# A block of adaLN, spectral filter and SwiGLU on one core: three products instead of four in the spectral stage, in groups of four, with loads and warming matmuls reordered

## The chip, the cores and the metric

The kernel runs on one core of a Trainium2 chip. The metric is the device time of one execution in microseconds (us). Five runs of the kernel before gave a median of 291.14 us (290.09 to 292.46). The engines are TensorE (PE; its weight loads are PEld), VectorE (DVE), ScalarE (ACT), GpSimd (POOL) and SyncE (SP, whose queue SPq issues the DMAs).

## The reference

The input x has 2048 rows of 640 numbers in bf16. The layer has two halves, each behind a layer norm that is scaled and shifted per column by values computed from a vector c. The first half is a filter in the frequency domain, the second a SwiGLU network with 1728 hidden columns.

```python
mod = (_silu(c) @ w_mod).reshape(c.shape[0], 6, 1, -1)      # sa, ca, ga, sb, cb, gb
h = _layernorm(x, axis=-1) * (1 + ca) + sa
x = x + ga * irfft2(rfft2(h) * (w_r + 1j * w_i))
h = _layernorm(x, axis=-1) * (1 + cb) + sb
x = x + gb * ((_silu(h @ w_gate) * (h @ w_up)) @ w_down)
```

The two-dimensional transform has 2048 frequencies along the rows and 321 along the columns; w_r and w_i have that shape.

## The kernel before

The kernel is one straight program; each engine executes its own instructions in the order in which the program lists them, and all DMAs are issued from the SP queue in order.

**Tables and splitting.** The transforms are matmuls with tables built on the host. The 640 columns are split by their remainder r modulo 4, so that a column transform gives frequencies l = 0 to 80 and four combinations of the r give the rest. The 2048 rows are split as 128 x 16: row 16p + t sits on partition p in tile t. So the row transform is one of length 128 (tables G and H, with tile-dependent twiddles) and one of length 16 (tables KS2 and KI inside Ktab).

**Front (lines 220 to 376).** The SP queue issues c, the part of w_mod for ca, the table R, then x and G in pieces, and then the spectral weights. Each weight plane is needed twice: as it is (Wn), and mirrored in rows and columns (Wv); `flip` copies a plane reversed in rows into DRAM, and `load_rev` reads it back. TensorE runs 34 warming matmuls (lines 267 and 268) that nothing uses. Line 357 turns c into a column, line 358 applies silu, `mod_cols` (line 277) multiplies it with a part of w_mod in 25 matmuls with one moving column each, and lines 367 and 368 scale R with 1 + ca.

**Forward loop (lines 377 to 403).** For each of 16 tiles, `t1` transposes x (lines 304, 305), `stats` gets its moments by matmul (line 315), `dfwd` applies the column transform (lines 284, 287), `zout` subtracts the mean on VectorE (line 339), `gscale` scales G by the reciprocal standard deviation on GpSimd, and `s1`, two tiles later, applies the 128-point row transform (lines 348 to 351) into PSUM banks 6 and 7, from which ScalarE casts into A_sb (line 352). In iteration 12 the modulation sa is computed into bank 6, and in iteration 14 sixteen matmuls with a filled table SL (line 402) make SA, the contribution of the shift sa to row frequency 0. Lines 404 and 405 negate the w_i planes.

**Spectral stage (lines 408 to 580).** It goes over the 81 values of l in groups of 8 (some smaller). A_sb has to be transposed for each l: for two groups and the pair 0, 80 by TensorE (`t2_pe`, line 439), for the rest by DMA transposes of 16 l each (`t2_dma`, line 420). Three of those are issued at the start, the fourth in iteration 4, behind the modulation weights and two tables; `sa_add` (line 462, GpSimd) then adds SA. `stage_a` (line 470) applies the 16-point row transform with KS2, 128 columns per l, two PSUM banks per group, two groups in turn; VectorE multiplies the result with the weights in four instructions per group (line 482). The four real products of a complex product are kept apart in PP, and `stage_b` (line 502) sums and transposes them by two accumulating matmuls per l with the identity. ScalarE casts that to Y2 (line 508), `stage_c` (line 517) applies the inverse 16-point transform, and ScalarE writes Em or Er (lines 521 to 526). `rot` (lines 536, 537) makes the rotated copy on GpSimd, for the last groups on VectorE. `mods2` computes ga, gb (line 544), sb and cb (line 277) in iterations 4 to 8, and multiplies the table RI with ga on GpSimd (line 552). TensorE's order in iteration g is stage b of g, `mods2`, stage a of g + 2, stage c of g - 1.

**Inverse transform (lines 646 to 687) and FFN (lines 698 to 769).** `s1inv` needs all groups of E; line 670 adds the residual. The FFN goes in chunks of 2, 4, 4, 4 and 2 tiles; its gate and up weights are loaded into the place of Wn and Wv (line 591) once the last product is done.

Of the kernel before, what the change touches and what calls it, by code (L numbers as in the profile page):

```python
# [24 lines left out]
NWARM = 34  # L25
# [5 lines left out]
def _tables():  # L31

# [37 lines left out]
    KS2 = np.zeros((16, 2, 4, 2, 2, 16, 2))  # L70
    KI = np.zeros((3, 2, 2, 16, 2, 16, 4, 2))
    for m in range(4):
# [3 lines left out]
        for r in range(4):  # L76
# [3 lines left out]
            KS2[:, :, r, hl, :, :, mm] = M.transpose(2, 0, 1, 3)  # L80
# [8 lines left out]
    K = np.zeros((128, 4, 128))  # L89
    K[:, 0, :] = KS2.reshape(128, 128)  # L90
    for v in range(3):
        K[:, 1 + v, :] = KI[v].reshape(128, 128)
# [44 lines left out]
def adaln_block_kernel(ctx, tc, A_x, A_w_r, A_w_i, B_x, B_w_gate, B_w_up, B_w_down, c, w_mod, out):  # L137
# [24 lines left out]
    Ktab = const.tile([P, 4, 128], BF16, name="Ktab")  # L162
    KS2 = Ktab[:, 0, :]
# [41 lines left out]
    SL = rL.cut(0, [2, 4, 2, 128])  # L205
# [36 lines left out]
    Wflip = [flip(A_w_i, "wflip_i"), flip(A_w_r, "wflip_r")]  # L242

    def load_rev(plane, f):
        nc.sync.dma_start(Wv[:, plane, :, :], f[:].rearrange("k p l -> p k l"))
# [21 lines left out]
    for i in range(NWARM):  # L267
        nc.tensor.matmul(banks(0, 1, [128]), lhsT=ones[:], rhs=ones[:], start=True, stop=True)
# [25 lines left out]
    if True:  # L294
# [49 lines left out]
        def s1(t, Z, Gs):  # L344
# [7 lines left out]
            nc.scalar.copy(A_sb[:, :, t, :, :].rearrange("p l c r -> p c l r"),  # L352
                           aps[:, :, :324].rearrange("p c (r l) -> p c l r", r=4))

        cps = psum[:, 6, 0:NC5]
        for k in range(NC5):
            nc.tensor.matmul(cps[:, k:k + 1], lhsT=c_row[0:1, k * 128:(k + 1) * 128], rhs=one11[:], start=True, stop=True)
        nc.scalar.activation(sc_f[:], cps, ACT.Silu)
# [4 lines left out]
        mod_cols(mps, wm_ca, True)  # L363
        t1(0)
        nc.vector.tensor_scalar_add(one_p_ca[:], mps, 1.0)
        for r in range(4):
            nc.vector.tensor_scalar_mul(Rs[:, 0, r, :], Rp[:, 0, r, :], one_p_ca[:, r:r + 1])
        nc.vector.tensor_scalar_mul(Rs[:, 1], Rp[:, 1], one_p_ca[:, 4:5])
        t1(1)
        stats(0)  # L370
# [6 lines left out]
        for t in range(NT + 2):  # L377
# [11 lines left out]
            if t == 12:  # L389
                mps = psum[:, 6, 0:NC5]  # L390
                mod_cols(mps, wm_sa, True)
                nc.vector.tensor_copy(sa_col[:], mps)
                for v in range(2):
                    src = sa_col[:, 0:4] if v == 0 else sa_col[:, 4:5].to_broadcast([P, 4])
                    nc.vector.tensor_copy(_rev(SL, 1024 * v, [[257, 4], [132, 2], [8, NT]]),
                                          src.unsqueeze(2).unsqueeze(3).to_broadcast([P, 4, 2, NT]))
            if t == 14:
                sps = psum[:, 6, 0:NL]
                for i in range(16):
                    v, r, c2 = i // 8, i // 2 % 4, i % 2  # L400
                    b0 = 81 * c2
                    nc.tensor.matmul(sps, lhsT=SL[:, v, r, c2, :], rhs=Rp[:, v, r, b0:b0 + 81], start=(i == 0), stop=(i == 15))
                nc.vector.tensor_scalar_mul(SA[:], sps, float(P))
        nc.vector.tensor_scalar_mul(Wn[:, 0], Wn[:, 2], -1.0)
        nc.vector.tensor_scalar_mul(Wv[:, 0], Wv[:, 2], -1.0)


    Em = rE.cut(0, [2, 64, 128])
# [410 lines left out]
```

## Time and profile before

| | us |
|---|---|
| median of five runs | 291.14 |
| the profiled execution | 290.19 |
| its span, first to last instruction | 288.3 |
| TensorE busy | 266.8 (93%) |
| VectorE busy | 150.1 (52%) |
| ScalarE busy | 111.4 (39%) |
| GpSimd busy | 44.7 (16%) |

A timeline row reads: start in us, length in us, engine, line, operation, output <- input, count, and in brackets how long the engine had been idle and what ended that. Rows of one line that follow each other are merged. A row of the stretches view gives for each engine the busy time and the number of instructions, and then the clock that was granted to TensorE (1.00 is full), the busy share of the 16 DMA engines, and GB/s. A row of the groups view ends with the busy time, the mean length of one instruction in ns, and the idle time before.

### The profile page before, as it was taken

How to read it: one execution, taken by the hardware profiler on the slowest of the kernel's cores; microseconds unless marked ns; L12 is line 12 of the kernel's file. 1: busy time of each engine (PE TensorE's matmuls, PEld its weight loads, DVE VectorE, ACT ScalarE, POOL GpSimd, SP SyncE). 2: the span in 40 equal slices, each digit the busy share in tenths (PEclk: the TensorE clock that was granted, in tenths of full speed). 3: DMA queues.
4: the chain of work that ended last, by engine and by line, in shares of the span. 5: the costliest groups of instructions: out<-in, count | busy, mean ns of one | idle time of the engine just before them, and what ended most of it. 6: DMA issues, size and time to landing. Idle time of an engine off the chain costs nothing.

```text
span 288.3 us, 5475 instructions
## 1 busy us (share of the span) xinstructions
PE 266.8 (93%) x2222; PEld 184.7 (64%) x2222; DVE 150.1 (52%) x346; ACT 111.4 (39%) x198; POOL 44.7 (16%) x87
## 2 busy tenths in 40 slices
PE   6899986993959999999999999999999999999995
PEld 6688854872858888764444774444675444678883
DVE  1377768992546877943862323863322742422422
ACT  2468734772677778214223103322203223202310
POOL 4167741335340100200020000020000100000000
PEclk9999999999888999999999999999999999999999
DMA  6999967999959300051004011004001020011001
GB/s 232 366 286 309 314 174 140 247 394 169 321 177 389 76 2 5 3 114 32 2 11 79 24 48 32 0 2 92 22 31 49 0 48 0 0 48 50 3 0 45
DMA packets 41575, 31.27 MB, mean 108 GB/s; under 512 B 20815, under 2 KB 37070, under 8 KB 41422
## 3 DMA queue, kind: packets, MB, share of 16 engines
q1 hardware_dynamic: 41550, 30.93, 37.7%
q8 instruction: 17, 0.28, 0.4%
q14 instruction: 8, 0.07, 0.1%
HBM read 23.35 MB, written 4.72 MB: 97 GB/s over the span
## 4 chain that ended last, share of the span: by engine, by line
PE 65%; DMA 2%; DVE 1%; ACT 1%; issue 0%; ACTq 0%
PE psum L715 19%; PE psum L718 19%; PE psum L760 19%; PE psum L650 3%; DMA rW<-rL 2%; PE psum L665 2%; PE psum L668 1%; PE psum L705 1%; ACT rW L641 1%; PE psum L652 1%; DVE rA L728 1%; DVE rL L626 0%; DVE rE L722 0%; ACT rL L655 0%; DVE rE L763 0%
## 5 line engine op out<-in xcount | busy, mean ns | idle before, releaser
L718 PE MATMUL psum<-rW 128*128 128x512 bf16 (+1 forms) x325 | 66.9, 336 | 0.0
L715 PE MATMUL psum<-rW 128*128 128x512 bf16 (+1 forms) x325 | 66.9, 336 | 0.0
L721 ACT ACTIVATE rE<-psum 128x512 f32<-128x512 f32 (+1 forms) x65 | 33.2, 511 | 68.4 <-PE psum L715 68.3
L715 PEld LDWEIGHTS <-rW 128*128 128x128 bf16 x325 | 31.8, 98 | 24.5
L718 PEld LDWEIGHTS <-rW 128*128 128x128 bf16 x325 | 31.8, 98 | 24.5
L722 DVE TENSOR_TENSOR rX<-psum,rE 128x512 bf16<-128x512 f32 x26 | 17.9, 688 | 29.9 <-PE psum L718 28.4
L722 DVE TENSOR_TENSOR rE<-psum,rE 128x256 bf16<-128x256 f32 (+1 forms) x39 | 19.9, 511 | 24.6 <-PE psum L718 22.6
L765 DVE TENSOR_TENSOR rE<-psum,rM 128x640 bf16<-128x640 f32 x15 | 12.4, 824 | 38.3 <-PE psum L760 38.3
L760 PE MATMUL psum<-rA,rE 128*128 128x320 bf16 x224 | 31.2, 299 | 0.7 <-DVE rA L728 0.6
L760 PE MATMUL psum<-rA,rX 128*128 128x320 bf16 x224 | 30.8, 299 | 0.0
L482 DVE TENSOR_TENSOR rM<-psum,rW 128x512 bf16<-128x512 f32 (+3 forms) x48 | 25.5, 604 | 8.3 <-PE psum L470 8.3
L760 PEld LDWEIGHTS <-rE 128*128 128x128 bf16 x224 | 21.9, 98 | 9.6 <-issue 0.6
L760 PEld LDWEIGHTS <-rX 128*128 128x128 bf16 x224 | 21.9, 98 | 8.8
L622 POOL TENSOR_TENSOR rstd<-rstd,mhalf 128x4 f32<-128x4 f32 (+1 forms) x5 | 4.4, 885 | 138.8 <-DVE rstd L618 106.8
L707 ACT ACTIVATE rE<-psum 64x512 f32<-64x512 f32 (+1 forms) x5 | 2.5, 505 | 48.1 <-PE psum L705 48.1
L339 DVE SCALAR_TENSOR_TENSOR rE<-rE,msum,psum 128x648 bf16<-128x648 f32 x16 | 14.2, 889 | 5.7 <-PE psum L287 5.1
L502 PE MATMUL psum<-identb,rM 128*128 128x128 bf16 x162 | 14.3, 236 | 1.8 <-DVE rM L482 1.6
L670 DVE TENSOR_TENSOR rM<-psum,rX 128x640 f32<-128x640 f32 x16 | 12.9, 815 | 5.9 <-PE psum L668 5.8
L502 PEld LDWEIGHTS <-rM 128*128 128x128 bf16 x162 | 12.3, 150 | 2.9 <-DVE rM L482 2.8
L352 ACT CAST rA<-psum 128x648 bf16<-128x648 f32 x16 | 11.2, 699 | 7.0 <-PE psum L351 5.7
L307 ACT COPY rE<-psum 128x640 bf16<-128x640 bf16 x16 | 10.9, 693 | 6.7 <-PE psum L305 6.7
L508 ACT CAST rL<-psum 128x512 bf16<-128x512 f32 (+2 forms) x21 | 11.1, 577 | 5.2 <-PE psum L502 5.2
(122 smaller groups left out, 345.2 us busy)
## 6 DMA issues: line engine op xcount, KB each, us to landing
rM<-in_w_mod_dram SPq DMA_DIRECT2D x4, 800.0 KB, 6.2
out_dram<-rE SPq DMA_DIRECT2D x16, 160.0 KB, 1.8
rA<-in_B_w_down_dram SPq DMA_DIRECT2D x1, 2080.0 KB, 8.4
rX<-in_A_x_dram SPq DMA_DIRECT2D x3, 640.0 KB, 8.9
rM<-in_w_mod_dram SPq DMA_DIRECT2D x1, 1600.0 KB, 11.6
rW<-in_B_w_gate_dram SPq DMA_DIRECT2D x1, 1440.0 KB, 10.0
rW<-in_B_w_up_dram SPq DMA_DIRECT2D x1, 1440.0 KB
rE<-tab_G SPq DMA_DIRECT2D x4, 256.0 KB, 8.1
```

The costliest lines, as they stand in the source:

```text
L339: nc.vector.scalar_tensor_tensor(Z[:].rearrange("p (h r) n -> p h (r n)", h=2), Cb[:].rearrange("p (h r) n -> p h (r n)", h=2), msum[:, t: ...
L352: nc.scalar.copy(A_sb[:, :, t, :, :].rearrange("p l c r -> p c l r"), aps[:, :, :324].rearrange("p c (r l) -> p c l r", r=4))
L482: nc.vector.tensor_tensor(PP[:, cp, hl, :, :, :, :n], in0, in1, ALU.mult)
L502: nc.tensor.matmul(yps[:, i - lo, :], lhsT=PP[:, cp, :, :, :, :, i].rearrange("p h a k m -> p (h a k m)"), rhs=identb[:], start=(cp == 0 a ...
L508: nc.scalar.copy(Y2[:, lo:hi, :], yps[:, :hi - lo, :])
L670: nc.vector.tensor_tensor(x1[:, t, :].rearrange("p (m h r) -> p m h r", h=2, r=2), ops[:, :, 0:320].rearrange("p h (r m) -> p m h r", r=2) ...
L715: nc.tensor.matmul(gu[:, 0, 0:N], lhsT=Wgu[:, 0, c5, fc * 128:(fc + 1) * 128], rhs=h2T[:, :, c5, :], start=(c5 == 0), stop=(c5 == NC5 - 1))
L718: nc.tensor.matmul(gu[:, 1, 0:N], lhsT=Wgu[:, 1, c5, fc * 128:(fc + 1) * 128], rhs=h2T[:, :, c5, :], start=(c5 == 0), stop=(c5 == NC5 - 1))
L721: nc.scalar.activation(sg[:], gu[:, 0, 0:N], ACT.Silu)
L722: nc.vector.tensor_tensor(AT[:, fc, :], gu[:, 1, 0:N], sg[:], ALU.mult)
L760: nc.tensor.matmul(ops4[:, h, 0:320], lhsT=AT[:, fc, tl * 128:(tl + 1) * 128], rhs=Wd_sb[:, fc, h * 320:(h + 1) * 320], start=(fc == 0), s ...
L765: nc.vector.tensor_tensor(xo[:].rearrange("p (h m) -> p h m", h=2), ops4[:, :, 0:320], x1[:, t, :].rearrange("p (h m) -> p h m", h=2), ALU ...
```

## The change

- **Three products.** The complex product of a spectrum value X = a + ib with a weight W = wr + i wi is formed from three real products: KS2 now yields a, -(a + b) and b - a (192 columns per l), and Wn and Wv hold three planes, the sum wr + wi, wi and wr. Real and imaginary part are sums of two of the three, with one product shared. The two that are not shared go together through one full matmul with the identity; the shared one is added by two matmuls of 64 output rows each, into the lower and the upper half of the PSUM partitions. The sums of the planes are made by `wsum` on VectorE, for Wn in iterations 10 to 13 and after the forward loop, for Wv inside the spectral stage.
- **Groups of four** l instead of eight: 21 groups, VectorE multiplying in two instructions per group. In the loop, stage a of g + 2 now stands ahead of stage b of g. Every fourth eviction of E goes to VectorE, the rotation is done for two groups at once, and the last group's eviction and rotation are halved.
- **Transposes and loads.** All four DMA transposes are issued first, then RI and H, then the rest of w_mod; its part for ga is loaded before the forward loop ends. The natural-order weights are loaded ahead of the flips. Four groups and the pair 0, 80 are transposed by TensorE.
- **Front.** c is loaded from ScalarE's queue, tile 0 of x ahead of R; the 34 warming matmuls of 128 columns are replaced by `idle_pe`, 3, 8, 1 and 2 matmuls of 512 columns at four places.
- **Modulation.** The matmuls for sa and SA move to the end of the forward loop, with banks of their own, and the last two of `mods2` for gb and those for sb and cb to the end of the spectral stage.

The core of the diff:

```diff
-NWARM = 34
+IDLE = (3, 8, 1, 2)
...
+            KS2[:, :, r, 0, hl, :, mm] = M[:, :, 0]
+            KS2[:, :, r, 1, hl, :, mm] = -M[:, :, 0] - M[:, :, 1]
+            KS2[:, :, r, 2, hl, :, mm] = M[:, :, 1] - M[:, :, 0]
...
-    nc.sync.dma_start(c_row[:], c)
+    nc.scalar.dma_start(c_row[:], c)
     nc.sync.dma_start(wm_ca[:], wm_v[:, :, D:2 * D])
+    nc.sync.dma_start(x_sb[:, 0:1, :], x_v[:, 0:1, :])
     nc.sync.dma_start(Rp[:], R_dram)
-    nc.sync.dma_start(x_sb[:, 0:2, :], x_v[:, 0:2, :])
+    nc.sync.dma_start(x_sb[:, 1:2, :], x_v[:, 1:2, :])
...
-    nc.sync.dma_start(Wn[:, 2, :, :], wi_v[:, :, 0:NW])
-    load_rev(2, Wflip[0])
+    nc.sync.dma_start(Wn[:, 1, :, :], wi_v[:, :, 0:NW])
+    nc.sync.dma_start(Wn[:, 2, :, :], wr_v[:, :, 0:NW])
+    Wflip = [flip(A_w_i, "wflip_i"), flip(A_w_r, "wflip_r")]
+    nc.sync.dma_start(Ktab[:], K_dram)
     nc.sync.dma_start(wm_sa[:], wm_v[:, :, 0:D])
-    nc.sync.dma_start(Ktab[:], K_dram)
-    nc.sync.dma_start(Wn[:, 1, :, :], wr_v[:, :, 0:NW])
-    load_rev(1, Wflip[1])
+    for i in range(2):
+        nc.sync.dma_start(Wv[:, 1 + i, :, :], Wflip[i][:].rearrange("k p l -> p k l"))
+    nc.sync.dma_start(wm_r[:, :, 0, :], wm_m[:, :, 0, :])
...
+    def idle_pe(n):
+        for i in range(n):
+            nc.tensor.matmul(banks(5, 1, [512]), lhsT=ones[:], rhs=ones[:].unsqueeze(1).to_broadcast([P, 4, 128]),
+                             start=True, stop=True)
...
+        def wsum(W, lo, hi, eng):
+            off = lo if W is Wn else NW - hi
...
+            eng.tensor_tensor(v[0], v[2], v[1], ALU.add)
...
+            if 10 <= t < 14:
+                wsum(Wn, 16 * t - 160, 16 * t - 144, nc.vector)
...
-        nc.vector.tensor_scalar_mul(Wn[:, 0], Wn[:, 2], -1.0)
-        nc.vector.tensor_scalar_mul(Wv[:, 0], Wv[:, 2], -1.0)
...
-        for bi in range(3):
+        for bi in range(4):
             t2_dma(bi)
...
         def stage_a(g):
-            xps = banks(2 + 2 * (g % 2), 2, [8, 128])
+            xps = banks(2 + 2 * (g % 2), 2, [4, 256])
...
-                nc.tensor.matmul(xps[:, i, :], lhsT=B2[:, j, :], rhs=KS2, start=True, stop=True)
+                nc.tensor.matmul(xps[:, i, 0:192], lhsT=B2[:, j, :], rhs=KS2, start=True, stop=True)
...
+                nc.vector.tensor_tensor(PP[:, :, hl], xv[:, :, hl], in1, ALU.mult)
...
+        def stage_b(g, PP):
+            yps = banks(g % 2, 1, [4, 128])
+            for i in range(n):
+                nc.tensor.matmul(yps[:, i, :], lhsT=_rev(PP, 64 * n + i, [[n, 128]]), rhs=identb[:], start=(i == 0), stop=False)
+            for i in range(n):
+                for a in range(2):
+                    nc.tensor.matmul(yps[64 * a:64 * a + 64, i, :], lhsT=_rev(PP, i, [[n, 64]]), rhs=identb[:], start=False,
+                                     stop=(i == n - 1))
...
+                if g % 4 == 3:
+                    nc.vector.tensor_copy(Ev, ev)
+                else:
+                    nc.scalar.copy(Ev, ev)
...
         for g in range(NG + 1):
+            if g + 2 < NG:
+                PPs[g + 2] = stage_a(g + 2)
+            sa_add(g + 4)
+            if g < NG:
+                Y2s[g] = stage_b(g, PPs.pop(g))
+            if g in (0, 2):
+                wsum(Wv, 16 * g, 16 * g + 32, nc.vector)
+            if 5 <= g < 7:
+                mods2(g - 5, 6 + g % 2)
             if g >= 1:
                 stage_c(g - 1, Y2s.pop(g - 1))
-                rot(groups[g - 1], nc.gpsimd if g < NG - 2 else nc.vector)
+            if g == NG - 2:
+                mods2(2, 2 + 2 * (NG % 2))
+            if g == NG - 1:
+                mods2(3, 3 + 2 * (NG % 2))
+        mods2(4, 2 + 2 * (NG % 2))
```

More of the change, by code (lines that the diff above doesn't have):

```diff
@@ L266, in adaln_block_kernel @@
     nc.scalar.activation(warm[:], warm[:], ACT.Silu)
-    for i in range(NWARM):
-        nc.tensor.matmul(banks(0, 1, [128]), lhsT=ones[:], rhs=ones[:], start=True, stop=True)
+    def idle_pe(n):
+        for i in range(n):
+            nc.tensor.matmul(banks(5, 1, [512]), lhsT=ones[:], rhs=ones[:].unsqueeze(1).to_broadcast([P, 4, 128]),
+                             start=True, stop=True)
+    idle_pe(IDLE[0])
     def mod_cols(ps_ap, w_ap, radix):
@@ L509, in stage_y @@
+            Y2 = rL.cut(12288 + 1024 * (g % 2), [4, 128])
+            nc.scalar.copy(Y2[:, 0:n, :], yps[:, 0:n, :])
             return Y2
```

198 lines of the change are left out of this document (87 added, 111 removed).

## The prediction

> **What bounds the kernel now.** I read the page first (span, granted clock), then cut the span into stages with the stretches view, then followed the timeline of TensorE, VectorE and the SP queue through the stages that the change touches, and took prices from the groups view.
>
> ```profile
> span 288.3 us, 5475 instructions
> ```
> ```profile
> core 0: us, PE busy (x) PEld busy (x) DVE busy (x) ACT busy (x) POOL busy (x), PEclk, DMA share, GB/s
> 1.08:13.00 11.92, 10.19 (x102) 8.94 (x103) 2.24 (x17) 3.31 (x6) 2.72 (x3) 1.00 0.90 311
> 13.00:35.00 22.00, 20.96 (x247) 17.59 (x246) 16.70 (x66) 17.28 (x25) 15.24 (x32) 1.00 1.03 312
> 44.24:65.00 20.76, 17.61 (x238) 15.21 (x239) 19.15 (x34) 13.30 (x22) 6.10 (x14) 1.00 1.04 275
> 65.00:70.83 5.83, 1.14 (x10) 0.56 (x9) 1.15 (x2) 1.71 (x4) 3.06 (x4) 1.00 0.99 182
> 70.83:74.40 3.57, 3.57 (x34) 3.41 (x35) 2.48 (x4) 1.61 (x3) 1.90 (x4) 0.55 0.81 243
> 74.40:85.48 11.08, 7.64 (x135) 6.50 (x133) 5.38 (x18) 8.43 (x14) 4.59 (x8) 0.96 0.73 220
> 85.48:88.20 2.72, 2.72 (x24) 2.57 (x25) 0.00 (x0) 1.06 (x2) 0.00 (x0) 0.50 1.07 370
> 105.70:288.30 182.60, 178.42 (x1124) 109.47 (x1121) 81.36 (x164) 47.50 (x95) 5.58 (x8) 1.00 0.12 29
> ```
>
> The FFN after 105.70 (182.60 us, TensorE busy 178.42) is untouched, and I carry it over. The spectral stage runs from 44.24 to 85.48, 41.24 us. It has three parts: up to 65 us VectorE is busy 19.15 of 20.76 us, so the products of line 482 set the pace; then almost six microseconds in which TensorE and VectorE do next to nothing; then work at a granted clock of 0.55, and at 0.50 again from 85.48, when the inverse transform has begun.
>
> ```profile
> 44.26 7.72 SPq L420 DMA_TRANSPOSE rL<-rA  x3
> ```
> ```profile
> 55.59 12.77 SPq L420 DMA_TRANSPOSE rL<-rA  x1
> ```
> ```profile
> 64.14 1.16 PE L502 MATMUL psum<-identb,rM 128*128 128x128 bf16 x16
> 70.83 0.75 PE L470 MATMUL psum<-Ktab,rL 128*128 128x128 bf16 x8 [4.59 <-POOL rL L462]
> 72.23 1.91 PE L502 MATMUL psum<-identb,rM 128*128 128x128 bf16 x16
> ```
>
> These rows show the hole: the fourth DMA transpose reaches the SP queue at 55.59, behind the tables and modulation weights, and occupies it for 12.77 us; line 462 on GpSimd waits for its data, and TensorE for line 462. After the 4.59 us wait sixteen matmuls of line 502 take 1.91 us instead of 1.16.
>
> **Front.** The small load of c goes to ScalarE's queue, ahead of its table load; the first tile of x goes ahead of the table R; the 34 small warming matmuls become 3 + 8 + 1 + 2 of 512 columns, spread between the real ones.
>
> ```profile
> 1.08 3.81 PE L268 MATMUL psum<-ones 128*128 128x128 bf16 x34 [1.08 <-DVE warm L259]
> 5.88 0.96 PE L277 MATMUL psum<-sc_col,rM 128*128 128x1 bf16 x25 [0.77 <-DMA rM<-in_w_mod_dram]
> 7.55 0.61 PE L304 MATMUL psum<-identb,rX 128*128 128x128 bf16 x4 [0.70 <-DMA rX<-in_A_x_dram]
> 9.05 0.72 PE L315 MATMUL psum<-rE 128*128 128x129 bf16 x5 [0.25 <-ACT rE L307]
> 12.27 0.63 PE L304 MATMUL psum<-identb,rX 128*128 128x128 bf16 x4
> 13.00 0.44 PE L304 MATMUL psum<-identb,rX 128*128 128x128 bf16 x4
> ```
> ```profile
> out_dram<-rE SPq DMA_DIRECT2D x16, 160.0 KB, 1.8
> ```
>
> Four transposes take 0.63 us at 12.27 and 0.44 at 13.00: TensorE is at its slow pace until then, although the clock column reads 1.00. At that pace 128 columns cost 3.81/34 = 0.112 us, so 512 cost 0.45. A transfer of 160 KB lands 1.8 us after its issue, so c is there by about 3.0 and holds up nothing. If the pace stays slow: the 8 matmuls after the c columns end near 3.0 + 3.6 = 6.6, 0.7 later than line 277 started before; 0.96 + 0.45 + two transposed tiles at about 0.55 each + 0.9 put the first stats matmul at 10.0, one microsecond late; but what follows it up to 13.00 (3.95 us slow, about 2.0 at the full pace) then runs fast: 12.2 against 13.0, a gain of 0.8. If the unbroken run from 3.0 gives the full pace by 6.5: 6.5 + 0.8 + 0.2 + 0.6 + 0.45 = 8.6, plus 2.0 is 10.6, a gain of 2.4. I take 1.5, the middle. The forward loop after it is TensorE's (busy 20.96 of 22.00 us from 13 to 35, in which 13 tiles pass, 1.69 each), so the lead is carried on.
>
> The Trainium skill (TensorE: Matmul & The Clock Gate, "The HAM clock gate") says that full clock comes after one window of about 3.4 us of sustained activity and that the window runs freely; the grid of changes here (13.00, 74.4 and 88.2 lie 18 and 4 times 3.41 us apart) agrees. By it the gain would lie anywhere between my two ends, from run to run.
>
> **Tail of the forward loop.** Two inserts move out of iterations 12 and 14, and the two negations (lines 404, 405) go; four sums of 512 elements come into iterations 10 to 13 on VectorE, and one at the end.
>
> ```profile
> 35.02 0.93 PE L277 MATMUL psum<-sc_col,rM 128*128 128x1 bf16 x25 [0.23 <-ACT rA L352]
> ```
> ```profile
> 36.27 0.30 PE L348 MATMUL psum<-rE 128*128 128x324 bf16 x1
> ```
> ```profile
> 37.77 0.30 PE L348 MATMUL psum<-rE 128*128 128x324 bf16 x1 [0.23 <-ACT rA L352]
> ```
> ```profile
> 39.28 0.78 PE L402 MATMUL psum<-rE,rL 128*128 128x81 bf16 x16 [0.23 <-ACT rA L352]
> 40.47 0.30 PE L348 MATMUL psum<-rE 128*128 128x324 bf16 x1 [0.41 <-DVE SA L403]
> ```
> ```profile
> 43.73 1.22 DVE L405 TENSOR_SCALAR rW<-rW 128x4096 bf16<-128x4096 bf16 x1
> ```
> ```profile
> 46.79 1.29 DVE L482 TENSOR_TENSOR rM<-psum,rW 128x512 bf16<-128x512 f32 x2 [1.25 <-PE psum L470]
> ```
>
> Here one s1 follows the other at 1.50 us undisturbed, but at 2.70 around the SA matmuls, which shared banks 6 and 7 with s1: the insert costs 1.2, and that in iteration 12 (0.23 + 0.93) about as much. After, the mod columns (0.96) run in bank 0 while s1(14) waits for its bank anyway, exposing about 0.6; the SA matmuls (0.78) run while ScalarE casts s1(15), hidden but for some 0.3. So 2.4 - 0.6 - 0.3 = 1.5 gained; ends 0.5 and 2. The four sums find VectorE idle for (22.00 - 16.70)/13 = 0.4 us of each tile, about what one costs (below), and s1 takes what VectorE makes two tiles later. The sum ahead of SA's eviction (0.4) lies beside TensorE's SA matmuls.
>
> **Spectral stage.** Each l now takes three products instead of four: stage a moves 192 columns instead of 128, stage b takes one full matmul and two with 64 output rows instead of two full ones, groups are of 4 instead of 8, and all four DMA transposes go first.
>
> ```profile
> 54.34 0.61 PE L470 MATMUL psum<-Ktab,rL 128*128 128x128 bf16 x8
> ```
> ```profile
> 59.18 0.84 PE L544 MATMUL psum<-rM,sc_rep 128*128 128x320 bf16 x5
> ```
> ```profile
> L482 DVE TENSOR_TENSOR rM<-psum,rW 128x512 bf16<-128x512 f32 (+3 forms) x48 | 25.5, 604 | 8.3 <-PE psum L470 8.3
> ```
> ```profile
> 63.67 2.48 DVE L482 TENSOR_TENSOR rM<-psum,rW 128x512 bf16<-128x512 f32 x4 [0.32 <-PE psum L470]
> ```
> ```profile
> 75.37 1.42 DVE L482 TENSOR_TENSOR rM<-psum,rW 128x256 bf16<-128x256 f32 x4 [1.27 <-PE psum L470]
> ```
> ```profile
> 77.33 1.39 PE L277 MATMUL psum<-sc_col,rM 128*128 128x1 bf16 x50
> ```
> ```profile
> L728 DVE TENSOR_TENSOR rA<-rA,gb_bc 128x640 bf16<-128x640 bf16 (+1 forms) x14 | 6.6, 478 | 0.0
> ```
> ```profile
> L524 ACT CAST rE<-psum 128x512 bf16<-128x512 f32 x2 | 1.2, 596 | 0.0
> ```
>
> VectorE: 512 elements cost 0.62, 256 cost 0.355, so 384 cost 0.49; 21 groups of two, some smaller, are 19.9 us against 25.5 before. To it come the sums of Wv (544 and twice 1,024 elements; at the rate of line 728 about 0.4 + 2 x 0.75 = 1.9, at one element a cycle of line 482 2.8), and every fourth eviction of E (0.6 each, four before the last product): 19.9 + 1.9 + 2.4, and 0.3 for the piece of l = 80, make 24.5. So VectorE gains only about a microsecond over before.
>
> TensorE: eight matmuls of 128 columns take 0.61 with 0.15 of drain, 0.0575 each; five of 320 take 0.84, 0.136 each; 192 come out at 0.084. Line 502's sixteen give 0.0625. No row shows a 64-row matmul. Below, one could cost nothing beside its partner (0.031 each); above, its weight load could stand exposed, 0.15 more, by the row in the rivals. I take 0.0625, the price of the nearest row, the full one. Per l: 0.084 + 3 x 0.0625 + 0.0575 = 0.329, times 81 = 26.6 (before: 0.24, 19.4). With 18 transposes (1.2), the gate matmuls (4 x 0.68) and the mod columns, now at the end (1.39), 31.9 us. TensorE becomes the bound, by 31.9 against 24.5. Unhidden: from the first transpose through ScalarE's copy to the first product (before 46.79 - 44.24 = 2.55 us, with VectorE held up by line 405 to 44.95; now about 1.7), the wait for it (1.0), and at the end one Y eviction and one halved E eviction behind matmuls (0.8): 3.5 in all. 31.9 + 3.5 = 35.4 against 41.24: 5.8 gained, ends 3 and 9. The hole of 4.59 us goes because transposes 1 to 3 took about 2.6 us each (7.72 us of queue for three): the fourth lands some 14 us after the start, and its group is due at about 24. What is late next is TensorE itself. GpSimd's queue gets RI's two multiplications behind RI's landing; rotations behind them are due only at the end. The FFN's weights still wait for the last product and keep their distance to the FFN, which hangs on it too.
>
> **Inverse transform.** Its first 2.72 us ran at 0.50; with mod columns issued just ahead and no hole, full pace halves that: 1.2 gained, ends 0 and 1.4.
>
> **Sum.** 1.5 + 1.5 + 5.8 + 1.2 = 10.0: span 278.3, with 1.89 around it (290.19 - 288.3) 280.2. The profiled execution lies 0.95 below the median 291.14, so the median comes to 281.1, say 281.0.
>
> **Rivals.**
>
> ```profile
> L502 PEld LDWEIGHTS <-rM 128*128 128x128 bf16 x162 | 12.3, 150 | 2.9 <-DVE rM L482 2.8
> ```
> ```profile
> 30.38 4.32 SPq L245 DMA_DIRECT2D rW<-wflip_r  x1
> ```
> ```profile
> rW<-wflip_r SPq DMA_DIRECT2D x1, 0.5 KB, 11.8
> ```
> *Half matmuls expose their weight loads* (slower). If a 64-row matmul cannot start its load under its predecessor, each of the 162 adds up to the 0.150 us of the strided load: 24 us, 305. It decides from 0.062 us exposed per half (10.0/162). For it: nothing in this trace uses half the array. Against: line 502's loads, at 0.150 each, hide in a spacing of 0.0625. Chance 0.07.
>
> *The array drains at each change of shape.* Stage b changes from full to half and back in all 21 groups. A matmul of line 470 leaves 0.15 us behind its issue; two per group are 42 x 0.16 = 6.7 us: 287.7. Nothing in the trace excludes it. Chance 0.20. The Trainium skill (TensorEngine Tiling (Array Packing), "Key Properties") states that changing the tiling mode drains TensorE; the same page says that the two halves can run in parallel. No run here shows either.
>
> *Pairs run side by side.* Two halves for the price of one save 81 x 0.0625 = 5.1; the stage's 35.4 comes to 30.3, which VectorE allows (1.7 + 24.5, and some 2.7 for the last group's way through b, Y, c and E: 28.9): 276. Chance 0.15.
>
> *Data is late.* Wv's last load is issued at 30.38 and lands 11.8 later, at 42.2, as the queue is busy throughout (1.03 from 13 to 35); the new order starts 0.4 earlier and makes Wv wait for the same data; the stage would start at 41.2 and want Wv by 43. Another 800 KB is queued ahead of the transposes, so they may not go first in fact. If either slips 2 us: 283. Chance 0.08.
>
> **How the numbers follow.** The forecast has 0.50; its own range, from the ends above, is 277.5 to 285. About 0.5% (1.5 us) is what a measurement here can tell from no change. The range 275.5 to 288 takes in the pairs and the drain and leaves out the exposed loads and the far ends, some 0.17. Faster: 0.50 + 0.15 + 0.08 + most of the drain, 0.16 = 0.89; slower 0.07; same 0.04.
>
> **What would show it.** Right: no wait of line 462's successor over 1 us; stretch from the first transposes to the first inverse matmul 34 to 38 us, TensorE busy about 32 of it; VectorE with idle time before the products; clock 1.00 at the start of the inverse; the forward loop's end near 41.2. Wrong: half matmuls with starts over 0.1 apart or gaps of 0.15 around them; a product waiting for a DMA of rW; the first stats matmul after 10.2 with no faster pace behind it; an FFN longer than 182.6.

## The result and the profile after

The changed kernel takes 280.73 us, the median of 9 runs (279.90 to 282.04); the kernel before, in 15 runs beside it, 291.14. The ratio is 0.9645, with a 95% interval of 0.9622 to 0.9667. The profiled execution took 280.76 us, so it stands for the median. Of its page the first line:

```profile
span 279.0 us, 5649 instructions
```

The span fell by 9.3 us, from 288.3. The stretches view of the changed kernel shows where (columns as in the prediction's first view):

```profile
13.83:38.75 24.92, 24.22 (x280) 19.43 (x278) 20.00 (x71) 17.48 (x26) 17.92 (x37) 1.00 1.03 288
40.07:45.00 4.93, 2.03 (x27) 1.76 (x27) 1.82 (x6) 2.46 (x4) 0.78 (x4) 1.00 1.26 276
45.00:48.30 3.30, 3.30 (x32) 2.58 (x31) 3.23 (x7) 0.59 (x1) 0.00 (x0) 0.52 0.99 175
48.30:60.00 11.70, 10.60 (x153) 8.94 (x149) 8.97 (x19) 8.40 (x16) 5.05 (x8) 0.99 1.07 244
60.00:70.00 10.00, 10.00 (x159) 8.75 (x158) 8.89 (x19) 7.46 (x14) 6.25 (x12) 1.00 1.05 381
76.91:79.63 2.72, 2.52 (x43) 2.24 (x40) 1.06 (x6) 1.29 (x2) 0.40 (x1) 1.00 1.08 393
96.26:279.00 182.74, 178.43 (x1123) 109.47 (x1121) 81.39 (x164) 47.54 (x95) 5.59 (x8) 1.00 0.12 29
```

The reader is to see three things. Between 60 and 70 us TensorE is busy all the time and VectorE is not: the bound of the spectral stage has moved to TensorE. The stage's first eight microseconds are poor: TensorE works 2.03 of 4.93 us, and then 3.30 us at a granted clock of 0.52. And the inverse begins at clock 1.00, where it had 0.50. The stretch at 0.52 belongs to the profiled execution: in four of the nine the mean granted clock was 1.00, and these took 279.90 to 281.10 us, against 280.51 to 282.04 for the other five.

The timeline of the changed kernel gives the reason for the poor start, the order of loads on the SP queue, what GpSimd does, and one group in the steady state:

```profile
32.34 4.44 SPq L257 DMA_DIRECT2D rW<-wflip_r  x1
...
40.32 11.59 SPq L444 DMA_TRANSPOSE rL<-rA  x3
52.02 2.16 SPq L444 DMA_TRANSPOSE rM<-rA  x1
54.23 0.74 SPq L450 DMA_DIRECT2D rH<-tab_RI  x1
```
```profile
43.89 0.46 DVE L374 TENSOR_TENSOR rW<-rW 128x544 bf16<-128x544 bf16 x1 [1.44 <-DMA rW<-wflip_r]
45.00 0.69 PE L487 MATMUL psum<-Ktab,rM 128*128 128x192 bf16 x4 [2.23 <-DVE rM L498]
57.87 2.76 POOL L565 TENSOR_TENSOR rH<-rH,ga_bc 128x640 bf16<-128x640 bf16 x2 [3.13 <-DMA rH<-tab_RI]
61.66 0.27 POOL L479 TENSOR_TENSOR rL<-rL,SA 128x16 bf16<-128x16 bf16 x1
...
58.07 0.49 PE L487 MATMUL psum<-Ktab,rL 128*128 128x192 bf16 x4
58.40 0.39 PE L505 MATMUL psum<-identb,rM 128*128 128x128 bf16 x4
58.72 0.46 PE L508 MATMUL psum<-identb,rM 128*64 128x128 bf16 x8
59.11 0.40 PE L520 MATMUL psum<-Ktab,rL 128*128 128x128 bf16 x4
59.34 0.49 PE L487 MATMUL psum<-Ktab,rL 128*128 128x192 bf16 x4
```

VectorE needs the sum of the mirrored planes for the first group, and waits 1.44 us for the mirrored wr to land at 43.89; TensorE waits 2.23 us for the product behind it. The mirrored wr is issued at 32.34, where the kernel before issued it at 30.38, and takes about as long to land. A group of four takes from 58.07 to 59.34, 1.27 us, without a gap. The four-microsecond hole around the fourth block is gone.

The landmarks of all profiled kernels, read off TensorE's timeline (start of the first row transform of the forward loop, of the first transpose of the spectral stage, of the first inverse matmul; the stage is the difference of the last two), with the medians:

| kernel | first row transform | stage starts | inverse starts | stage | median us |
|---|---|---|---|---|---|
| before | 16.60 | 44.24 | 85.48 | 41.24 | 291.14 |
| changed | 13.83 | 40.07 | 76.91 | 36.84 | 280.73 |
| before, fourth transpose first | 16.98 | 45.16 | 88.40 | 43.24 | 292.93 |
| before, new front | 14.13 | 44.26 | 86.07 | 41.81 | 292.81 |
| before, both | 14.26 | 44.89 | 87.28 | 42.39 | 293.31 |
| before, hole gone | 16.59 | 44.54 | 81.42 | 36.88 | 286.39 |
| changed but four products | 14.13 | 40.65 | 78.70 | 38.05 | 283.18 |
| changed, tables late | 13.87 | 40.09 | 86.05 | 45.96 | 290.38 |
| changed, old front | 16.95 | 43.18 | 77.65 | 34.47 | 281.29 |
| changed, idle matmuls out | 14.86 | 41.08 | 76.72 | 35.64 | 280.84 |
| changed, flips first | 14.13 | 44.19 | 78.28 | 34.09 | 282.38 |
| changed, two full matmuls | 14.13 | 40.38 | 74.69 | 34.31 | 279.30 |
| flips first, sums late, two full | 14.19 | 40.28 | 74.72 | 34.44 | 277.68 |
| the same, gate late | 14.14 | 40.22 | 73.59 | 33.37 | 277.64 |

Kernels with the same front differ by up to 0.4 us in the first column (16.59 to 16.98 with the old one, 13.83 to 14.26 with the new one and its idle matmuls), so a landmark's difference of that size says little.

### The profile page after: what moved, and what is told of

Same layout as the page of the kernel before. It is cut to its first block, busy times and chain, and to the rows that moved or that the text cites. A ratio compares the mean times of both kernels' runs of the same rounds, so it can differ in the third digit from the quotient of the medians.

```text
span 279.0 us, 5649 instructions
## 1 busy us (share of the span) xinstructions
PE 266.8 (96%) x2283; PEld 181.6 (65%) x2283; DVE 149.8 (54%) x353; ACT 109.8 (39%) x202; POOL 46.0 (16%) x90
## 4 chain that ended last, share of the span: by engine, by line
PE 75%; DMA 9%; SPq 8%; DVE 3%; ACT 2%; issue 1%; ACTq 0%; DVEq 0%
PE psum L731 20%; PE psum L734 20%; PE psum L776 19%; DMA rW<-wflip_r 4%; SPq L252 3%; PE psum L508 3%; DMA rE<-tab_G 2%; PE psum L487 2%; PE psum L520 2%; SPq L244 2%; PE psum L666 2%; DMA rW<-rL 2%; PE psum L681 2%; PE psum L505 2%; SPq L242 1%; PE psum L684 1%
## 5 line engine op out<-in xcount | busy, mean ns | idle before, releaser
L731 PEld LDWEIGHTS <-rW 128*128 128x128 bf16 x325 | 31.8, 98 | 24.5
L734 PEld LDWEIGHTS <-rW 128*128 128x128 bf16 x325 | 31.8, 98 | 24.5
L498 DVE TENSOR_TENSOR rM<-psum,rW 128x384 bf16<-128x384 f32 (+2 forms) x42 | 20.9, 548 | 3.4 <-PE psum L487 3.3
L511 ACT CAST rL<-psum 128x512 bf16<-128x512 f32 (+2 forms) x21 | 12.0, 572 | 9.4 <-PE psum L508 9.2
L671 ACT CAST rL<-psum 128x640 bf16<-128x640 f32 x16 | 10.9, 690 | 5.1 <-PE psum L668 3.3
L364 ACT CAST rA<-psum 128x648 bf16<-128x648 f32 x15 | 10.5, 700 | 5.5 <-PE psum L361 4.2
L642 DVE TENSOR_SCALAR rL<-rM,st,rstd 128x640 bf16<-128x640 f32 x16 | 9.7, 625 | 0.5 <-POOL rstd L638 0.5
## 6 DMA issues: line engine op xcount, KB each, us to landing
rW<-in_B_w_up_dram SPq DMA_DIRECT2D x1, 1440.0 KB, 12.2
```

Of the source, the lines that this page charges most:

```text
L498: nc.vector.tensor_tensor(PP[:, :, hl], xv[:, :, hl], in1, ALU.mult)
L511: nc.scalar.copy(Y2[:, 0:n, :], yps[:, 0:n, :])
L671: nc.scalar.copy(VT[:], vps[:, 0:5, :])
L731: nc.tensor.matmul(gu[:, 0, 0:N], lhsT=Wgu[:, 0, c5, fc * 128:(fc + 1) * 128], rhs=h2T[:, :, c5, :], start=(c5 == 0), stop=(c5 == NC5 - 1))
L734: nc.tensor.matmul(gu[:, 1, 0:N], lhsT=Wgu[:, 1, c5, fc * 128:(fc + 1) * 128], rhs=h2T[:, :, c5, :], start=(c5 == 0), stop=(c5 == NC5 - 1))
```

## The experiments

My theory after the first look: the hole is worth its 4.6 us and the front its 2.8, so that most of the gain can be had with four products. The rival: the gain hangs on the three products. The kernel before had medians of 291.70, 291.61, 291.38 and 291.17 us in the four batches of runs.

### What the hole was

**The fourth transpose alone.** The kernel before, with the fourth DMA transpose issued right behind the first three; its block gets a place of its own, and the products two buffers instead of three.

```diff
-        for bi in range(3):
+        for bi in range(4):
             t2_dma(bi)
...
-            if g == 4:
-                t2_dma(3)
```

> The kernel before, with one thing changed: the fourth DMA transpose is issued right behind the first three, into a buffer of its own (the product buffers go from three to two to make room). Theory A (the hole and the slow stretch behind it were the cost of the old spectral stage, the number of products was not): 4.6 us of hole and 1.7 of slow pace go, some 0.8 at the start of the inverse: 284 to 285. Theory B (the old stage was bound by VectorE's four products, and the hole only hid part of that): VectorE and the later loads take up most of the room, 288 or more.

292.93 us, a ratio of 1.0024 (0.9991 to 1.0056): nothing. The timeline of this kernel:

```profile
70.08 2.74 POOL L552 TENSOR_TENSOR rH<-rH,ga_bc 128x640 bf16<-128x640 bf16 x2 [4.14 <-DMA rH<-tab_RI]
72.78 0.27 POOL L462 TENSOR_TENSOR rM<-rM,SA 128x16 bf16<-128x16 bf16 x1
73.10 1.03 PE L470 MATMUL psum<-Ktab,rM 128*128 128x128 bf16 x8 [4.49 <-POOL rM L462]
```

The block has long landed, but its addition (line 462) stands in GpSimd's queue behind the multiplication of RI (line 552), and that waits 4.14 us for RI, which is loaded behind all of the modulation weights. The same two rows of the kernel before:

```profile
66.19 2.74 POOL L552 TENSOR_TENSOR rH<-rH,ga_bc 128x640 bf16<-128x640 bf16 x2 [2.61 <-DMA rH<-tab_RI]
70.51 0.27 POOL L462 TENSOR_TENSOR rL<-rL,SA 128x16 bf16<-128x16 bf16 x1 [1.58 <-DMA rL<-rA]
```

There the block landed 1.58 us after line 552 was done. So the hole had two causes, one behind the other, and I had seen only the last.

**Both, front and hole.** The same with the new front.

```diff
-            if g == 4:
-                t2_dma(3)
...
-NWARM = 34
+IDLE = (3, 8, 1, 2)
```

> Both edits together on the kernel before, with four products in groups of eight and the old place of the SA matmuls. Theory A: the gains add, 291.1 - 6.5 - 2.8 = 282, within 1.5 us of the changed kernel, so the three products themselves bring next to nothing. Theory B: 286 or more, the rest being the products' own.

293.31 us, 1.0055 (1.0025 to 1.0085). The hole stood as before (TensorE waited 4.83 us for GpSimd at 72.45), and the front's lead did not reach the stage either.

**The addition moved forward.** The first experiment, with one change more: GpSimd adds to a block one group earlier, so ahead of line 552 in its queue.

```diff
-            sa_add(g + 1)
+            sa_add(g + 2)
```

> The first experiment again (fourth transpose issued right behind the first three), and GpSimd adds the mean's term to a block one group earlier in its queue, ahead of its two multiplications by the gate. Theory A (the hole of the kernel before was this addition's place in GpSimd's queue, behind a multiplication that waited for a table, and TensorE has no other wait there): TensorE's 4.5 us wait goes, about 287 us against 291.7. Theory B (GpSimd or VectorE is late anyway and the wait comes back at the next group or at the end of the stage): 290 or more.

286.39 us, 0.9818 (0.9787 to 0.9850), 5.2 us less than the kernel before. Its timeline:

```profile
60.23 0.27 POOL L462 TENSOR_TENSOR rM<-rM,SA 128x16 bf16<-128x16 bf16 x1
69.41 2.76 POOL L552 TENSOR_TENSOR rH<-rH,ga_bc 128x640 bf16<-128x640 bf16 x2 [4.08 <-DMA rH<-tab_RI]
67.82 0.61 PE L470 MATMUL psum<-Ktab,rM 128*128 128x128 bf16 x8
```

GpSimd still waits 4.08 us for RI, and nobody minds: TensorE takes the block at 67.82 without a wait. With four products in groups of eight the stage now takes 36.88 us, as long as the changed kernel's.

**The tables late.** The changed kernel, with RI and H loaded behind the modulation weights as before.

```diff
-        nc.sync.dma_start(RI[:], RI_dram)
-        nc.sync.dma_start(Htab[:], H_dram)
         nc.sync.dma_start(wm_r[:, :, 3, :], wm_m[:, :, 3, :])
         nc.sync.dma_start(wm_r[:, :, 1:3, :], wm_m[:, :, 1:3, :])
+        nc.sync.dma_start(RI[:], RI_dram)
+        nc.sync.dma_start(Htab[:], H_dram)
```

> The changed kernel with the two tables of the inverse (RI and H) loaded behind the modulation weights again, as in the kernel before. Theory A (GpSimd's queue is what counts: the addition to the third block stands behind the multiplications of RI, which would then wait for the table): RI lands some 7 us later, TensorE waits 4 us or more for a block, 284 to 287 us. Theory B (with all four transposes first and the additions four groups ahead the table's place does not matter): 280 to 281.5 us.

290.38 us, 0.9956 (0.9940 to 0.9973): with these two loads behind, 9.65 of the 10.4 us are lost. Timeline and one stretch of this kernel:

```profile
65.77 2.74 POOL L565 TENSOR_TENSOR rH<-rH,ga_bc 128x640 bf16<-128x640 bf16 x2 [10.91 <-DMA rH<-tab_RI]
69.54 0.27 POOL L479 TENSOR_TENSOR rL<-rL,SA 128x16 bf16<-128x16 bf16 x1
69.86 0.82 PE L487 MATMUL psum<-Ktab,rL 128*128 128x192 bf16 x4 [7.67 <-POOL rL L479]
```
```profile
69.86:72.65 2.79, 2.79 (x24) 2.36 (x25) 1.02 (x2) 0.88 (x2) 1.06 (x2) 0.50 1.12 334
```

TensorE waits 7.67 us and then works 2.79 us at half clock, which costs some 1.4 more: together the 9.1 us by which the stage grew. The forecast of 284 to 287 priced only the wait, and that too low. The gains do not add up one by one: the additions moved forward gave 5.2 us without any change to the tables. One edit takes the addition out from behind the wait for RI, the other shortens that wait.

### What became of the lead

**New front alone**, on the kernel before.

```diff
-NWARM = 34
+IDLE = (3, 8, 1, 2)
...
-    nc.sync.dma_start(c_row[:], c)
+    nc.scalar.dma_start(c_row[:], c)
...
+    nc.sync.dma_start(x_sb[:, 0:1, :], x_v[:, 0:1, :])
     nc.sync.dma_start(Rp[:], R_dram)
```

> The kernel before with the new front alone: c on ScalarE's queue, tile 0 of x ahead of the table R, 3 + 8 + 1 + 2 warming matmuls of 512 columns, the order of the scalings of R. If the lead of 2.8 us at the first row transform is carried through: 288.3. If the loads of the weights then hold the spectral stage up by as much, or the fourth transpose's queue does: 290 to 291.

292.81 us, 1.0027 (0.9994 to 1.0060). The first row transform starts 2.47 us earlier, the stage at the same time: in iteration 12 the lead is given back. From this kernel's timeline:

```profile
35.01 0.95 PE L283 MATMUL psum<-sc_col,rM 128*128 128x1 bf16 x25 [2.70 <-DMA rM<-in_w_mod_dram]
```

The matmuls for sa wait for their part of w_mod. The changed kernel has them in the last iteration, where the data are there.

**The idle matmuls out.** The changed kernel without the eight long matmuls behind the columns of c.

```diff
-IDLE = (3, 8, 1, 2)
+IDLE = (3, 0, 1, 2)
```

> The changed kernel without its eight long idle matmuls behind the columns of c, so that TensorE pauses between the first columns and the modulation columns. Theory A (the front's gain of 2.8 us comes from TensorE's unbroken work up to the full pace at about 4.2 us): the pace stays slow for up to 7 us more, the first row transform starts at 15 to 16.6 in place of 13.83, and the time is 281.7 to 283.5 against 280.7. Theory B (the gain comes from the early load of c and the order of the loads): first row transform at or before 14.2, 280 to 281.2 us.

280.84 us, 0.9629 (0.9598 to 0.9660). Timeline:

```profile
5.78 0.96 PE L287 MATMUL psum<-sc_col,rM 128*128 128x1 bf16 x25 [3.02 <-DMA rM<-in_w_mod_dram]
...
8.90 0.65 PE L325 MATMUL psum<-rE 128*128 128x129 bf16 x5
9.38 0.30 PE L294 MATMUL psum<-rE 128*128 128x324 bf16 x1
...
14.86 0.31 PE L358 MATMUL psum<-rE 128*128 128x324 bf16 x1
```

The full pace comes at about 9.3 us and the row transform at 14.86, 1.03 later than in the changed kernel: between the two theories, nearer to A. The time says B: the inverse starts at 76.72, as early as before. The stage begins later, finds the mirrored weights landed, and has neither the wait nor the slow stretch.

**The old front.** The front's loads and warming matmuls as before, in the changed kernel; only the order in which R is scaled stays.

```diff
-IDLE = (3, 8, 1, 2)
+NWARM = 34
...
-    nc.scalar.dma_start(c_row[:], c)
+    nc.sync.dma_start(c_row[:], c)
...
-    nc.sync.dma_start(x_sb[:, 0:1, :], x_v[:, 0:1, :])
     nc.sync.dma_start(Rp[:], R_dram)
```

> The changed kernel with the front of the kernel before (34 small warming matmuls, c on SP's queue, the first two tiles of x behind the table R). Theory A (the front's lead of 2.8 us is used up by the wait for the reversed weights, which land at 43.9 us whenever the loop ends): first row transform at about 16.6, stage start at about 42.8, no wait for the weights, first inverse matmul within 0.8 us of the changed kernel's 76.91, 280.5 to 282 us against 280.7. Theory B (the lead is kept): 283 to 284 us.

281.29 us, 0.9674 (0.9636 to 0.9713). The stage starts 3.1 us later than the changed kernel's and the inverse 0.74 later. Its stage as one stretch, and that of the changed kernel:

```profile
43.18:77.65 34.47, 31.55 (x493) 27.08 (x494) 26.64 (x57) 23.53 (x44) 16.21 (x31) 1.00 1.09 278
```
```profile
40.07:76.91 36.84, 32.84 (x493) 27.95 (x494) 27.01 (x57) 23.53 (x44) 16.19 (x31) 0.95 1.08 288
```

For the same 493 matmuls the changed kernel has 1.3 us more of busy time, at clock 0.95, and 1.1 us more of waiting: 2.4 us of the lead is paid back to the late load.

**Flips first.** The changed kernel with the mirrored copies issued ahead of the plain weights.

```diff
+    Wflip = [flip(A_w_i, "wflip_i"), flip(A_w_r, "wflip_r")]
     nc.sync.dma_start(Wn[:, 1, :, :], wi_v[:, :, 0:NW])
     nc.sync.dma_start(Wn[:, 2, :, :], wr_v[:, :, 0:NW])
-    Wflip = [flip(A_w_i, "wflip_i"), flip(A_w_r, "wflip_r")]
```

> The changed kernel with the three-part flips issued ahead of the natural-order weights, as in the kernel before; everything else as changed. If the order of the loads makes Wv late (the SP queue stands still until the second flip has landed): the wait of VectorE for Wv (1.4 us) and of TensorE behind it (2.2 us) go, and with them the slow stretch of 3.3 us at a clock of 0.52: 277 to 278.5. If the amount of data is what counts (the DMA engines are busy to 1.0 all the way): Wv lands when it did, 280.5 to 281.

282.38 us, 0.9684 (0.9634 to 0.9734), slower than either forecast. The stage shrinks to 34.09, and the forward loop ends 4.1 us later. Timeline of VectorE:

```profile
33.11 0.43 DVE L374 TENSOR_TENSOR rW<-rW 128x512 bf16<-128x512 bf16 x1 [3.25 <-DMA rW<-in_A_w_r_dram]
```

Now the plain wr is late for the sums in iteration 10, and they stand ahead of the loop's own work on VectorE. The order of the loads chose only where to wait.

### What the three products brought

**Four products.** The kernel before with everything else: the front, the order of loads, sa and SA at the loop's end, four transposes first, the tables early, the additions forward; products and groups as before. Of its edits, beside those shown:

```diff
-            if t == 12:
-                mps = psum[:, 6, 0:NC5]
+            if t == NT - 1:
+                mps = psum[:, 0, 0:NC5]
                 mod_cols(mps, wm_sa, True)
...
+        nc.sync.dma_start(RI[:], RI_dram)
+        nc.sync.dma_start(Htab[:], H_dram)
         nc.sync.dma_start(wm_r[:, :, 3, :], wm_m[:, :, 3, :])
         nc.sync.dma_start(wm_r[:, :, 1:3, :], wm_m[:, :, 1:3, :])
-        nc.sync.dma_start(RI[:], RI_dram)
-        nc.sync.dma_start(Htab[:], H_dram)
```

> The kernel before with everything of the change but the three products and the groups of four: the new front, the order of the loads, the mean's matmuls at the end of the forward loop, four transposes first, the table of the inverse early, the block's addition early. Theory A (front 2.8, tail 1.4 and hole 4.5 us are worth what the traces show, and the three products bring the small rest): 282 to 284 us. Theory B (the stage's gain hangs on the three products and groups of four, as VectorE's four products a group of eight set the pace without them): 286 or more.

283.18 us, 0.9696 (0.9649 to 0.9742): theory A. Against the 280.73 of the change, the three products, the groups of four and the new order at the stage's end bring 2.45 us of some 10.4. The size is rough: the four runs lie in two pairs, 282.25 and 282.51, 283.85 and 284.00, and the profile is of the slowest. In it about 1.0 lies in the inverse; the stretches view of this kernel:

```profile
78.70:81.42 2.72, 2.72 (x24) 2.58 (x25) 0.00 (x0) 1.06 (x2) 0.00 (x0) 0.50 1.09 380
```

Without a hole the inverse still begins at half clock in this profile. In the kernel with late tables, hole and all, it runs from 86.05 to 105.39, 19.34 us, as in the changed kernel (19.35). So the hole does not decide. What differs just ahead of the inverse is that TensorE stood idle for 1.41 us in this kernel and works without a break in the changed one, where the modulation columns come last; that it is these columns no run tests alone.

**Two full matmuls.** The changed kernel with its planes in the order wi, sum, wr: the shared product lies in the middle, and a window of 128 columns over the first two and one over the last two do what one full matmul and two halves did.

```diff
             for i in range(n):
-                for a in range(2):
-                    nc.tensor.matmul(yps[64 * a:64 * a + 64, i, :], lhsT=_rev(PP, i, [[n, 64]]), rhs=identb[:], start=False,
-                                     stop=(i == n - 1))
+                nc.tensor.matmul(yps[:, i, :], lhsT=_rev(PP, i, [[n, 128]]), rhs=identb[:], start=False, stop=(i == n - 1))
```

> The changed kernel with its three planes in the order (imaginary, sum, real), so that the shared product lies between the other two and the transform back needs two matmuls of 128 columns a bin in place of one of 128 columns and two of 64; the result is the same. Theory A (in the spectral stage TensorE sets the pace at 1.27 us a group of four, and the eight half matmuls cost 0.39 of it where four full ones cost 0.22 to 0.32): 0.07 to 0.17 us off each of 21 groups, until VectorE (8.89 of 10.00 us busy, 1.13 a group) is what is late, so 278 to 279.5 us against 280.7 for the changed kernel, and TensorE waits for VectorE in the stage. Theory B (halves cost half, so nothing is gained): 280.5 to 281.5.

279.30 us, 0.9593 (0.9544 to 0.9642). A group in this kernel's timeline:

```profile
64.04 0.49 PE L487 MATMUL psum<-Ktab,rL 128*128 128x192 bf16 x4
64.37 0.39 PE L505 MATMUL psum<-identb,rM 128*128 128x128 bf16 x4
64.59 0.39 PE L507 MATMUL psum<-identb,rM 128*128 128x128 bf16 x4
64.81 0.39 PE L518 MATMUL psum<-Ktab,rL 128*128 128x128 bf16 x4
65.04 0.49 PE L487 MATMUL psum<-Ktab,rL 128*128 128x192 bf16 x4
```

1.00 us a group in place of 1.27. What the halves cost shows in their single starts. The stretches view of the changed kernel for line 508 alone counts the matmuls in flight (the first bracket; none of the eight has ended yet):

```profile
58.70:58.73 0.03, 0.01 (x2) 0.01 (x2) 1.00 0.76 273
58.73:58.82 0.09, 0.09 (x2) 0.09 (x4) 1.00 0.22 91
58.82:58.84 0.02, 0.02 (x4) 0.02 (x6) 1.00 0.00 0
58.88:58.90 0.02, 0.02 (x6) 0.02 (x6) 1.00 1.14 410
58.94:58.97 0.03, 0.03 (x8) 0.03 (x4) 1.00 0.70 273
```

They start in pairs: in the trace the two halves of a pair are 0.003 us apart, and the later pairs follow each other at 0.059, where full matmuls follow at 0.056. So a pair costs about what a full matmul does. What costs is the change of shape: the first half starts 0.150 behind the last full matmul, the second pair 0.106 behind the first, and stage c 0.157 behind the last half and its own second matmul 0.068 on, about 0.25 us a group above the even pace. That is nearly all of the 0.27. The stage gave 2.5 us (36.84 to 34.31), the median 1.4; TensorE, busy 28.08 of 34.31 us there, is no longer the only bound.

### A faster version

**Flips first, sums late, two full matmuls.** The two last ideas together; the sums of the plain weights move from iterations 10 to 13 to 14 to 17, where the late wr no longer holds up the loop.

```diff
-            if 10 <= t < 14:
-                wsum(Wn, 16 * t - 160, 16 * t - 144, nc.vector)
+            if 14 <= t < 18:
+                wsum(Wn, 16 * t - 224, 16 * t - 208, nc.vector)
```

> The changed kernel with the reversed weights' copies issued ahead of the plain weights, the sums of the plain weights moved to the last four iterations of the forward loop, and the order of planes of two full matmuls. Theory A (the wait for the reversed weights, 1.4 us on VectorE and 2.2 on TensorE with the slow clock behind it, goes without holding up the loop, and the halves' cost goes as well): 275 to 278 us. Theory B (the DMA engines are full until 43 us, so some other load is late by as much): 279 to 282.

277.68 us, 0.9525 (0.9486 to 0.9563): below both kernels. In its timeline the old mechanism is back, as TensorE has become faster than GpSimd's queue:

```profile
56.52 2.76 POOL L563 TENSOR_TENSOR rH<-rH,ga_bc 128x640 bf16<-128x640 bf16 x2 [4.25 <-ACT rE L535]
60.30 0.27 POOL L479 TENSOR_TENSOR rL<-rL,SA 128x16 bf16<-128x16 bf16 x1
60.62 0.50 PE L487 MATMUL psum<-Ktab,rL 128*128 128x192 bf16 x4 [2.14 <-POOL rL L479]
```

**Gate late.** The same, with the multiplications of RI moved to group 13, behind the last addition.

```diff
-                if i == 1:
-                    for v in range(2):
-                        nc.gpsimd.tensor_tensor(RI[:, v], RI[:, v], ga_bc[:], ALU.mult)
...
+            if g == 13:
+                for v in range(2):
+                    nc.gpsimd.tensor_tensor(RI[:, v], RI[:, v], ga_bc[:], ALU.mult)
```

> The version with the reversed weights first and two full matmuls, and GpSimd's two multiplications of the inverse's table by the gate moved from group 6 to group 13, behind the mean's additions to the last two blocks. Theory A (what held TensorE there for 2.1 us at 58.5 is again an addition that stands in GpSimd's queue behind these multiplications): the wait goes, about 275.5 to 276.5 us against 277.7. Theory B (the block's data land late, or VectorE is late anyway): 277 to 278.5 us.

277.64 us, 0.9517 (0.9497 to 0.9536). The 2.14 us wait is gone, but the median did not move: the range of theory B. The profile of the version before it, with the 2.14 us wait, is of its slowest run (278.92 against a median of 277.68), so that wait need not be in every run. In this profile TensorE waited 1.94 us for the first block's data at 49.01, and the stretch behind it ran below full clock; whether that is what ate the gain in all runs the runs do not settle.

## Why the prediction was right, point by point

**The sum.** 281.0 was forecast, 280.73 measured; 10.0 of span against 9.3. That it came so near is in good part luck: the front gave 1.27 us more than forecast, the stage 1.40 less and the inverse 0.33 less, and inside the stage two rivals came true that cancel each other. The range of 277.5 to 285 does not follow from the ends either; added up, they give 276.3 to 286.8.

**Front: 1.5 forecast (0.8 to 2.4), 2.77 measured, outside its range.** Two steps failed. I let the c columns come at about 3.0; they ran at 2.48, without a break behind the first idle matmuls. And I set the full pace at 6.5 at the earliest, counted from 3.0; the unbroken run began at 1.08. The eight idle matmuls took 2.62 us; at 0.45 slow and 4 x 0.0575 = 0.23 fast that is the full pace from about 4.3. (The lower end has a slip of its own: 10.0 and 2.0 are 12.0, not 12.2.) That the forward loop carries the lead on was right; that the lead shortens the kernel was not: undoing the front costs 0.56 us by the medians (281.29 against 280.73), too little for these runs to tell from no change, as the next stage waits for a load.

**Tail: 1.5 forecast, 1.40 measured** (44.24 to 40.07 is 4.17, less 2.77).

**Spectral stage: 5.8 forecast (3 to 9), 4.40 measured.** The step that failed is that "data is late" stood among the rivals, at 0.08, as an alternative. It came on top: the same term that pulled the stage forward made the late load decide. I had both numbers (weights wanted by 43, landing at 42.2) and took a margin of about one microsecond for safe, while both ends moved the wrong way: the weights were wanted at 42.45 and landed at 43.89. The load was to be issued 0.4 us earlier than before; it was issued 1.96 later (32.34 against 30.38). A product that waits for a DMA of rW stood among my signs of being wrong, and it came. Where nothing is late, with the old front, the stage takes 34.47; the forecast was 35.4. TensorE is busy 31.55 us there, and 31.9 was worked out; VectorE 26.64 against 24.5.

**The hole.** That it goes was right, the reason only half. "Rotations behind them are due only at the end" overlooked that the additions of line 479 stand behind RI's multiplications as well. I gave the early load of RI no price at all, and it decides over 9.65 us. The forecast came out because the change moved that load too.

**Prices on TensorE.** 1.316 us a group was forecast, 1.27 measured. Stage b was priced at 12 x 0.0625 = 0.75 and takes 0.32 + 0.39 = 0.71, but for another reason: four full matmuls at 0.056, four pairs at about 0.059, and 0.25 for the change of shape and back. The price of a half was wrong by a factor of two, and what it left out made up for it.

**Rivals.** Exposed loads: pairs 0.059 apart exclude them. Pairs side by side (chance 0.15) and the drain (0.20) stood as alternatives, and both came true. A pair at 0.059 in place of 2 x 0.0625 saves 81 x 0.066 = 5.3 us, where 5.1 was worked out; the change of shape, which I had called the drain, takes 21 x 0.25 = 5.3, where 6.7 was. They cancel, which is luck; and starts 0.15 apart around the halves were among my signs of being wrong. The Trainium skill (TensorEngine Tiling (Array Packing), "Key Properties") states both that a change of tiling mode drains TensorE and that tiles can execute in parallel; the trace agrees with both, at 0.25 us for a change and back and 0.003 us between the starts of two halves.

**Inverse: 1.2 forecast, 0.87 measured** (20.22 us from 85.48 to 105.70, 19.35 from 76.91 to 96.26). The half clock at its start is gone; "no hole" had no part in that, as the kernel with late tables has the hole and the full pace. Of the two reasons that I gave, the modulation columns right ahead of it remain, untested alone.

**FFN.** 182.60 before, 182.74 after: carried over, as forecast.

## What to carry to other kernels

When a stall ends with an engine that executes in order, read everything that stands ahead of the released instruction in its queue: here a multiplication whose result nobody needed for more than 15 us held up a small addition that TensorE was waiting for, and mending the visible cause alone gained nothing. A lead won early in a kernel is worth only what the next late transfer lets through, so set the landing time of every load against the new start of its reader and add the shortfall to the sum instead of listing it as a rival. An arithmetic saving (three products for four) moved the bound from VectorE to TensorE and was the smaller part of the gain; the order of loads and queues was the larger. And a price that comes out right for a group can hide two errors that cancel: look at the starts of single instructions before you trust it.

## What the runs showed of the hardware

- Two accumulating matmuls into the two halves of the output partitions start 0.003 us apart, and pair follows pair at 0.059 us where full matmuls follow each other at 0.056 (changed kernel, clock 1.00). Going from full matmuls to halves and back costs about 0.25 us in all: 0.150 instead of 0.056 to the first half, 0.106 instead of 0.059 to the second pair, 0.157 instead of 0.059 from the last half to the next full matmul, and 0.068 instead of 0.056 between the first two full matmuls after it.
- In the profiled runs a wait of TensorE in the stage was followed by some three microseconds at about half clock (0.52 behind 2.23 us in the changed kernel, 0.50 behind 7.67 us with the late tables), so that it cost about 1.4 to 1.6 us beyond its length. Behind the 2.14 us wait (flips first, sums late, two full) the matmuls kept their full pace for one microsecond more and ran at 0.51 from 61.63 to 64.50. The wait of 2.70 us in the forward loop (new front alone) had no such stretch behind it. The runs do not show what decides.
- In the front, the full pace came about 3.2 us after TensorE's start where it worked without a break (from 1.08 to 4.3), and about 3.5 us after the end of a pause (5.78 to 9.3). The Trainium skill (TensorE: Matmul & The Clock Gate, "The HAM clock gate") gives about 3.4 us of sustained activity; both lie near it.
